# Attention with forgetting gates and a SwiGLU block on one core: fillers on their own tile, other heads' logs sent early, constants by ScalarE, a new order

## The chip, the cores and the metric

The kernel runs on one NeuronCore of one Trainium2 chip. A core has five engines with a program each: TensorE (PE, matmuls; its weight loads are shown apart as PEld), VectorE (DVE), ScalarE (ACT), GpSimd (POOL) and SyncE (SP). Each runs its program in order, and they wait for each other by semaphores. SP, ACT and POOL also issue DMA transfers. The metric is the device time of one execution in microseconds (us); lower is better. A time given for a kernel is the median of its runs.

## What is computed

The inputs are q, k and v of shape (8 batches, 8 heads, 576 positions, 64) and a gate f in (0.8, 1.0) of shape (8, 8, 576). The reference, cut to what matters:

```python
scores = (q @ k.transpose(0, 1, 3, 2)) / 8
cum = np.cumsum(np.log(np.clip(f, 1e-4, 1.0)), axis=-1)
scores = scores + cum[..., :, None] - cum[..., None, :]      # decay
scores = np.where(causal, -1e9, scores)                      # no later key
attn = softmax(scores)
x = (attn @ v).transpose(0, 2, 1, 3).reshape(4608, 512)
g = x @ w_gate                                               # 512 x 1536
out = (g * sigmoid(g) * (x @ w_val)) @ w_out                 # 1536 x 512
```

So attention gives 4608 tokens of 512 features, and a gated feed-forward block follows.

## The kernel before, in words

All matmuls are in bfloat16 with sums in float32. A planner written in Python (class `Plan`) holds every step as an operation with an engine, an estimated duration, its predecessors, the buffers that it takes and a key. It plays the program through once: whenever an engine is free, it takes the ready operation with the lowest key, and the instructions are recorded in that order. The table `ORDER` at the end gives most operations a key; `T_SW`, `TWARM`, `QUAD0` and other constants are the planner's estimates. Once recorded, the order on every engine and every DMA queue is fixed. The planner puts fillers on PE (`dummy`, L995) where it expects PE to wait: matmuls whose result nobody reads.

The feed-forward part works in nine tiles of 512 tokens. For each of twelve blocks of 128 hidden features, `gate` (L892) multiplies the tokens by w_gate and w_val, ACT takes a tanh (L896), DVE forms the product in two steps (L900, L903), and `project` (L907) sums over the blocks into the output (L911, L914). In the first tile the first four blocks are done in two halves of 256 tokens, so that they can begin before all of batch 0 is through attention. The weights come in chunks on POOL's queue; in the first chunk there are four blocks.

Attention works by heads. Keys lie on partitions, queries on columns; a head's causal scores fill four banks of at most 512 columns. PE forms the scores (`score2` for batch 0, L708 to L720; `score` for the others, L690), ACT takes the exp (`expo`, L724), POOL clears the part above the diagonal (`mask`, L733), PE multiplies by v with a column of ones (`weigh`, L747), DVE divides by that column's sum (L754, L759), PE transposes (`flip`, L764), and the result is put into xT, the transposed tokens (L325 or L323).

For batches 0 and 1, q and k are loaded four heads at a time in "quads" (`ld_quad`, L541) by POOL, transposed by PE (`turn_two`, L549, for batch 0; `turn`, L565, for batch 1) and copied to their place in QK by ACT or DVE (L323, L325: the straightenings). Later batches go through DRAM and a transposing DMA.

The gates: `gates` loads f of the first 16 heads into 64 partitions, four copies of 16 rows (`ld_f`, four transfers, two each from SP and ACT), clips it on DVE (L355), takes the log on ACT (L358) into 128 partitions, and DVE forms the running sum (L362) and splits it into three bfloat16 parts in KG (L367 to L378); the columns are done in two parts, 256 and 320. `up` (L382) and `choose` (L387, L389) make the query side of the decay. `dec_in` (L399) writes eight small pieces of KG as extra rows of QK for batch 1; four more small writes fill rows of ones from the tile `ones` (L477). The other 48 heads are loaded flat, 128 x 216; after clip and log, `regroup` writes them to DRAM (L352) and reads them back a head per row (L350); DVE sums (L362) and splits them (`later`), and they go to DRAM (`dec_out`) for batches 2 and on.

Several constants are written once: the small factors `ct` and `one`, the padding of PT (L462), the ones beside v in three buffers VB (L505, L507), and the tile `ones` (L466).

## Time and profile before

| | us |
|---|---|
| median of 3 runs | 383.37 |
| lowest and highest run | 382.79, 384.94 |
| the profiled execution | 382.61 |
| its span, first to last instruction | 380.9 |
| PE busy in the span | 372.1 |
| DVE, ACT, POOL busy | 218.8, 211.2, 141.2 |

A row of a timeline gives the start in us from the span's start, the length, the engine, the line, the operation, what is written and read, and the number of instructions merged; in brackets stands the idle time of the engine before it and what ended it. A matmul's length includes the time until its result is out, so that the lengths of neighbours overlap. A row of the table by stretch gives busy times in a window. The chain of work that ended last is followed back from the last instruction through what released each step.

### The profile page before, as it was taken

The page shows a single profiled execution, that of the slowest core. Times are in us where ns is not written, and L with a number is a line of the kernel's source. Part 1 is how long each engine was busy: PE and PEld are TensorE (multiplying, and loading weights), DVE is VectorE, ACT ScalarE, POOL GpSimd, SP SyncE. Part 2 cuts the span into 40 slices and gives each one's busy share as a digit, 9 for nine tenths or more (in the row PEclk, how much of TensorE's full clock was granted, in tenths as well). Part 3 has the DMA queues.
Part 4 walks back from the last instruction along what each step waited for, and adds up shares of the span by engine and source line. Part 5 has one row for each costly group of instructions (what it writes and reads, how often), then busy time and mean ns, then how long its engine had stood idle before and what let it go on. Part 6 is the DMA issues. An engine that isn't in the chain of part 4 may idle for free.

```text
span 380.9 us, 8367 instructions
## 1 busy us (share of the span) xinstructions
PE 372.1 (98%) x3127; PEld 206.4 (54%) x3127; DVE 218.8 (57%) x458; ACT 211.2 (55%) x433; POOL 141.2 (37%) x368
## 2 busy tenths in 40 slices
PE   5999999999999999999999999999999999999997
PEld 3668555555555555545554565555654444444444
DVE  7899794467616772387327651576327815743860
ACT  5999745266566574835674577547763323323322
POOL 8896446236443463526452356513430000000000
PEclk9999999999999999999999999999999999999999
DMA  9999997997588989999799979992321011002003
GB/s 129 187 194 201 211 209 150 167 235 143 117 194 162 207 130 161 206 188 183 129 203 203 178 123 187 234 220 55 94 74 45 0 57 55 0 29 83 3 0 111
DMA packets 125319, 51.96 MB, mean 136 GB/s; under 512 B 112110, under 2 KB 119726, under 8 KB 124510
## 3 DMA queue, kind: packets, MB, share of 16 engines
q1 hardware_dynamic: 108782, 36.18, 47.8%
q0 software_dynamic: 16288, 15.14, 26.6%
q8 instruction: 24, 0.39, 0.4%
q14 instruction: 17, 0.14, 0.1%
q10 hardware_dynamic: 208, 0.11, 0.1%
HBM read 38.56 MB, written 17.07 MB: 146 GB/s over the span
## 4 chain that ended last, share of the span: by engine, by line
PE 89%; DMA 5%; ACT 2%; DVE 2%; issue 1%; POOL 1%; DVEq 0%; POOLq 0%
PE ps L892 46%; PE ps L907 25%; PE ps L690 9%; PE ps L747 7%; DMA lnf_d<-ot 4%; DMA QK<-lnf_d 1%; ACT PT L724 1%; PE ps L995 1%; PE ps L708 1%; PE ps L764 0%; DVE th L900 0%; ACT QK L323 0%; POOL xT L541 0%; PE ps L549 0%; DVE QK L362 0%
## 5 line engine op out<-in xcount | busy, mean ns | idle before, releaser
L896 ACT ACTIVATE th<-ps 128x512 f32<-128x512 f32 (+1 forms) x112 | 65.1, 582 | 83.9 <-PE ps L892 82.8
L892 PE MATMUL ps<-xT,wg 128*128 128x512 bf16 (+1 forms) x448 | 111.4, 371 | 0.2 <-DVE th L900 0.2
L892 PE MATMUL ps<-xT,wv 128*128 128x512 bf16 (+1 forms) x448 | 111.4, 371 | 0.1
L900 DVE SCALAR_TENSOR_TENSOR th<-th,ps 128x512 f32<-128x512 f32 (+1 forms) x112 | 74.6, 666 | 60.2 <-ACT th L896 59.8
L907 PE MATMUL ps<-wo,hh 128*128 128x512 bf16 (+3 forms) x468 | 105.8, 362 | 0.0
L724 ACT ACTIVATE PT<-ps 128x512 bf16<-128x512 f32 (+2 forms) x192 | 91.7, 510 | 18.6 <-PE ps L690 12.1
L903 DVE TENSOR_TENSOR hh<-th,ps 128x512 bf16<-128x512 f32 (+1 forms) x112 | 74.7, 668 | 11.8 <-PE ps L892 0.9
L733 POOL TENSOR_SCALAR_AFFINE_SELECT PT<-PT 128x128 bf16<-128x128 bf16 (+1 forms) x192 | 53.2, 282 | 55.5 <-ACT PT L724 50.4
L892 PEld LDWEIGHTS <-wv 128*128 128x128 bf16 x448 | 42.7, 97 | 41.6 <-issue 0.5
L690 PE MATMUL ps<-QK 68*128 68x256 bf16 (+4 forms) x392 | 64.8, 260 | 0.1
L892 PEld LDWEIGHTS <-wg 128*128 128x128 bf16 x448 | 42.3, 97 | 40.5 <-issue 0.5
L907 PEld LDWEIGHTS <-hh 128*128 128x128 bf16 x468 | 41.2, 97 | 34.4
L733 POOL TENSOR_SCALAR_AFFINE_SELECT PTa<-PTa 128x256 bf16<-128x256 bf16 x64 | 26.5, 418 | 85.3 <-ACT PTa L724 84.1
L754 DVE RECIPROCAL rc<-ps 128x5 f32<-128x5 f32 (+2 forms) x68 | 12.9, 190 | 68.3 <-PE ps L747 68.1
L911 ACT ACTIVATE ot<-ps 128x512 f32<-128x512 f32 (+3 forms) x39 | 22.0, 565 | 45.2 <-PE ps L907 43.7
L747 PE MATMUL ps<-VB,PT 128*128 128x65 bf16 x768 | 45.1, 193 | 0.0
L747 PEld LDWEIGHTS <-PT 128*128 128x128 bf16 x768 | 36.8, 97 | 14.4 <-POOL PT L733 1.3
L690 PEld LDWEIGHTS <-QK 68*128 68x128 bf16 x392 | 31.4, 97 | 17.2 <-issue 0.4
L724 ACT ACTIVATE PTa<-ps 128x384 bf16<-128x384 f32 x64 | 30.8, 488 | 14.3 <-PE ps L690 13.2
L759 DVE TENSOR_TENSOR xn<-ps,rc 128x320 bf16<-128x320 f32 (+2 forms) x72 | 32.2, 453 | 2.1
L325 POOL CAST VB<-natv 128x512 bf16<-128x512 f32 (+1 forms) x32 | 19.7, 631 | 0.0
L747 PEld LDWEIGHTS <-PTa 128*128 128x128 bf16 x192 | 13.1, 97 | 11.3 <-issue 1.1
(71 smaller groups left out, 153.2 us busy)
## 6 DMA issues: line engine op xcount, KB each, us to landing
out_dram<-ot SPq DMA_DIRECT2D x35, 256.0 KB
natv<-in_v_dram SPq DMA_DIRECT2D x25, 256.0 KB
qk_d<-in_q_dram POOLq DMA_DIRECT2D x24, 144.0 KB, 3.8
qk_d<-in_k_dram POOLq DMA_DIRECT2D x24, 144.0 KB, 4.4
wg<-in_moe_w_gate_dram POOLq DMA_DIRECT2D x3, 512.0 KB, 12.1
wv<-in_moe_w_val_dram POOLq DMA_DIRECT2D x3, 512.0 KB, 13.5
wo<-in_moe_w_out_dram POOLq DMA_DIRECT2D x4, 384.0 KB, 16.7
xT<-in_q_dram POOLq DMA_DIRECT2D x4, 288.0 KB, 8.8
```

The costliest lines, as they stand in the source:

```text
L325: E[e].tensor_copy(dst, src)
L690: nc.tensor.matmul(s[:, c : c + w], QK[:KR, hqk[p].i, 1, j * S + kt * P : j * S + (kt + 1) * P], QK[:KR, hqk[p].i, 0, j * S + q0 : j * S + ...
L724: nc.scalar.activation(place(h, i)[:, OFFS[i] : OFFS[i] + c], ps(bs)[:, :c], AF.Exp, scale=0.125)
L733: nc.gpsimd.affine_select(out=d, in_=d, pattern=pat, compare_op=ALU.is_ge, fill=0.0, base=0, channel_multiplier=-1,)
L747: nc.tensor.matmul(o[:, lo : lo + D + 1], pt[:, c : c + P], VB[hvb[b].i][:, kt, hb, : D + 1], start=first and n == 0, stop=last and n == l ...
L759: nc.vector.tensor_mul(XN[bx.i][:, qb : qb + nq, j], o, r)
L892: nc.tensor.matmul(ps(bf)[:, :n], w[:, ko, fc * P : (fc + 1) * P], xT[:, ko, t0 : t0 + n], start=(ko == 0), stop=(ko == KD - 1))
L896: nc.scalar.activation(TH[bt.i][:, :n], ps(bf)[:, :n], AF.Tanh, scale=0.5)
L900: nc.vector.scalar_tensor_tensor(out=t, in0=t, scalar=1.0, in1=ps(bf)[:, :n], op0=ALU.add, op1=ALU.mult)
L903: nc.vector.tensor_mul(HH[bh.i][:, lo : lo + n], TH[bt.i][:, :n], ps(bf)[:, :n])
L907: nc.tensor.matmul(ps(bf)[:m, c], HH[hs[fc].i][:, lo : lo + m], wo[:, fc, c], start=(fc == 0), stop=(fc == KF - 1))
L911: nc.scalar.activation(OT[bo.i][:m, c], ps(bf)[:m, c], AF.Copy, scale=0.5)
```

## The change

Five things are changed together, and the table `ORDER` is replaced, so that the order on all engines and queues is another.

The fillers multiply a tile of their own, `idle`, which DVE sets to ones at the start, and not the identity that POOL makes. The planner may place them from 0.8 us on (`ID_AT`, before 2.72); there are 38 and not 22. f of the first 16 heads is read in two transfers, one from SP and one from ACT, each writing 32 partitions from the same 16 rows read twice. The write of the other heads' logs to DRAM has the key -50 and may be planned from 6 us on (before 1 and 21), the read back from 16 us on (before 27). The ones of `VB[1]`, its zeros, and the tile `ones` may be written by ScalarE, with an activation of scale 0 and the constant as bias (`fill32`), and are. The recorded order has POOL issue two quads of q, one of k, a block of v and the second quad of k first, then the rest of v, then a chunk of w_val and one of w_gate ahead of batch 1's quads. On SP the four writes of rows of ones and the logs' write now stand ahead of the eight writes of gate rows, and the logs' read after the fifth of these. PE does all transposes of batch 0 before the scores of the second pair of heads, and those of batch 1 after the first gate block. The number of useful matmuls is the same.

Estimates of the planner are changed too: PE's half speed counts for transposes and ends at 7.0 and not 7.5 us, transposes of batch 0 take 0.22 and not 0.41, f is delayed by 0.7 and not 0.2 after its issue, small SP writes take 0.64 and not 0.45. A second part of the cheaper gate rows for the scores (`ONEHOT1`, `QS[1]`) is written but empty.

```diff
-                        if o.tag[0] != "turn":
-                            dur *= self.clock(t)
+                        dur *= self.clock(t)
...
+    idle = sb("idle", [P, P], BF16)
...
-    QS = xT[:, 3, 3 * S + D : 3 * S + D + HALF]
+    QS = [xT[:, 3, 3 * S + D : 3 * S + D + HALF], xT[:, 0, 2 * S : 3 * S - HALF]]
...
-        E[e].dma_start(out=lf[2 * H * c : 2 * H * (c + 1)], in_=f.rearrange("b h s -> (b h) s")[: 2 * H])
+        src = bass.AP(f.tensor, f.offset, [[0, 2], [S, 2 * H], [1, S]])
+        E[e].dma_start(out=lf[4 * H * c : 4 * H * (c + 1)], in_=src)
...
-        lds = [op(("ACT" if n % 2 else "SP", 0.45), ld_f, n, key=-40, dma=0.1, packet=100, tag="f") for n in range(4)]
-        ld1 = op(("SP", 0.5), ld_f, None, key=-39, dma=LD1, packet=50, ready=LD1_AT, behind=lds[2:3], tag="f1")
+        lds = [op(("ACT" if n else "SP", 0.6), ld_f, n, key=-40, dma=0.2, packet=100, tag="f") for n in range(2)]
+        ld1 = op(("SP", 0.5), ld_f, None, key=-39, dma=LD1, packet=50, ready=LD1_AT, behind=lds[:1], tag="f1")
...
-        a = op(("SP", 0.5), regroup, False, after=[l1], key=1, dma=0.5, packet=40, ready=21, tag="regroup")
+        a = op(("SP", 0.5), regroup, False, after=[l1], key=-50, dma=0.5, packet=40, ready=6, tag="regroup")
         regrouped.append(a)
-        l1 = [l1, op(("SP", 0.5), regroup, True, after=[a], key=1, dma=0.4, packet=100, ready=27, tag="regroup")]
+        l1 = [l1, op(("SP", 0.5), regroup, True, after=[a], key=2, dma=0.4, packet=100, ready=16, tag="regroup")]
...
+    def fill32(e, t, x):
+        if e == "ACT":
+            z = ct[:, 0:1]
+            src = bass.AP(z.tensor, z.offset, [[z.ap[0][0], t.shape[0]]] + [[0, n] for n in t.shape[1:]])
+            nc.scalar.activation(t, src, AF.Copy, scale=0.0, bias=x)
+        else:
+            E[e].memset(t, x)
...
-            E[e].memset(ones.bitcast(F32), ONE2)
+            fill32(e, ones.bitcast(F32), ONE2)
...
-                nc.vector.memset(VB[what][:, :, :, D:].bitcast(F32), ONE2)
+                fill32(e, VB[what][:, :, :, D:].bitcast(F32), ONE2)
             if what:
-                nc.vector.memset(VB[0 if what == "rest" else what][LAST:, NB - 1], 0.0)
+                fill32(e, VB[0 if what == "rest" else what][LAST:, NB - 1].bitcast(F32), 0.0)
...
+    op(("DVE", 0.12), lambda e: nc.vector.memset(idle.bitcast(F32), ONE2), key=-1e5)
...
-    o_vb = [op(("DVE", 0.4 if i else 0.12), blank, i, key=(-29.5, VB1_KEY)[i] if i < FIRST else 40 + 2000 * i, ready=0 if i == 0 else 10 if i < FIRST else 15) for i in range(NVB)]
+    o_vb = [op({"DVE": 0.4, "ACT": 0.6} if i == 1 else ("DVE", 0.4 if i else 0.12), blank, i, after=[o_ct] if i == 1 else [], key=(-29.5, VB1_KEY)[i] if i < FIRST else 40 + 2000 * i, ready=0 if i == 0 else 4.5 if i < FIRST else 15) for i in range(NVB)]
...
-    o_ones = op(ONES, blank, "ones", key=ONES_KEY, ready=10)
+    o_ones = op(ONES, blank, "ones", after=[o_ct], key=ONES_KEY, ready=4.5)
...
-        nc.tensor.matmul(z[:, :HALF], ident, ident.unsqueeze(1).to_broadcast([P, 2, P]), start=True, stop=True)
+        nc.tensor.matmul(z[:, :HALF], idle, idle.unsqueeze(1).to_broadcast([P, 2, P]), start=True, stop=True)
...
-TWARM = 7.5
-ID_AT = 2.72
+TWARM = 7.0
+ID_AT = 0.8
...
-QUAD0 = (1.85, 1.25, 1.65, 1.4)
+QUAD0 = (1.55, 1.45, 1.5, 1.4)
...
+ONEHOT1 = ()
...
-ONES = ('DVE', 0.3)
+ONES = {'DVE': 0.3, 'ACT': 0.32}
...
 ORDER = {
-    0: -76.058, 1: -665.8079, 2: -126.6589, 3: -127.6642, 4: 17.8158, 5: -127.6652, 6: -370.9327, 7: -665.8069, 8: -315.3735,
+    0: -1162.0513, 1: 132.4814, 2: -34.2406, 3: -978.2224, 4: -24.6101, 5: -24.6111, 6: -185.9564, 7: 238.587, 8: 241.7308, 9: 245.9194,
...
```

More of the change, by code (lines that the diff above doesn't have):

```diff
@@ L188, in run @@
                         taken[k] += 1
-                        push(max(end + (0.2 if o.tag == "f" else 0.9), T_SW if e == "POOL" else 0.0), "queue", o)
+                        push(max(end + (0.7 if o.tag == "f" else 0.9), T_SW if e == "POOL" else 0.0), "queue", o)
                         push(busy[e], "wake", None)
@@ L216 @@
 PACE_A = 8.8
-PACE0 = 58.0
+PACE0 = 57.0
 LEAD = 14.0
@@ L381, in up @@
     def up(e, c):
-        nc.scalar.activation(QS, cum[:, c], AF.Copy, scale=8.0)
+        nc.scalar.activation(QS[c.start > 0], cum[:, c], AF.Copy, scale=8.0)
     def choose(e, jj, c):
@@ L434, in gates @@
             a = op(("DVE", 0.1 + w * 0.00155), low, c, after=[a], key=kk, tag="low")
-            u = op(("ACT", 0.15 + w / 1100), up, c, after=[s], key=kk, tag="up") if i == 0 and ONEHOT else None
-            done.append([[a, o_one, u] if jj in ONEHOT and not i else
+            u = op(("ACT", 0.15 + w / 1100), up, c, after=[s], key=kk, tag="up") if (ONEHOT, ONEHOT1)[i] else None
+            done.append([[a, o_one, u] if jj in (ONEHOT, ONEHOT1)[i] else
                          [a, op({"ACT": 0.26 + w / 1100, "DVE": 0.08 + w / 960}, choose, jj, c, after=[s, o_one], key=PICK_KEY[i][jj], tag=("pick", i, jj))]
@@ L642, in four @@
                 bt = Buf("t", ("f", TURN_F))
-                o2 = op(("PE", 0.41), turn_two, jj, x, bt, after=[o1[x], o_id], take=[bt], key=kk, tag=("turn", 0, jj, x))
+                o2 = op(("PE", 0.22), turn_two, jj, x, bt, after=[o1[x], o_id], take=[bt], key=kk, tag=("turn", 0, jj, x))
                 turns.append(o2)
@@ L714, in score2 @@
                 o, keys = ps(bs[u])[:, c : c + w], KG_ALL[r, kt * P : (kt + 1) * P]
-                if i or jj not in ONEHOT:
+                if jj not in (ONEHOT1 if i else ONEHOT):
                     nc.tensor.matmul(o, keys, QG[jj][r, q0 : q0 + w], start=False, stop=end)
@@ L719, in score2 @@
                     nc.tensor.matmul(o, keys, one[r, jj : jj + 1].to_broadcast([D, w]), start=False, stop=False)
-                    nc.tensor.matmul(o, ident[r, mine : mine + 1].to_broadcast([D, P]), QS[r, q0 : q0 + w], start=False, stop=end)
+                    nc.tensor.matmul(o, ident[r, mine : mine + 1].to_broadcast([D, P]), QS[i > 0][r, q0 - (HALF if i else 0) : q0 - (HALF if i else 0) + w], start=False, stop=end)
     def expo(e, h, i, bs):
@@ L828, in attention2 @@
                     segs = [x[2] for x in BANKS[i]]
-                    cost = mm(*segs) * (3 if not i and jj in ONEHOT else 2) + 0.105
+                    cost = mm(*segs) * (3 if jj in (ONEHOT1 if i else ONEHOT) else 2) + 0.105
                     gate_rows = [o_past] + dec0[0][jj] + (dec0[1][jj] if i else [])
```

4 lines of the change are left out of this document (2 added, 2 removed), and 103 rows, old and new, of the table ORDER.

## The prediction, made before the changed kernel was run

> **What bounds the kernel now.** I read the table of busy time by stretch first, then the timeline of each engine over the first 50 us, then the chain of work that ended last.
>
> ```profile
> 0.00:60.00 60.00, 53.88 (x742) 35.99 (x743) 51.09 (x156) 45.42 (x100) 42.42 (x95) 1.00 1.24 188
> 60.00:378.20 318.20, 318.18 (x2387) 170.37 (x2385) 167.68 (x303) 165.51 (x333) 98.75 (x274) 1.00 0.66 127
> 378.20:380.90 2.70, 0.00 (x0) 0.00 (x0) 0.00 (x0) 0.22 (x1) 0.00 (x0) 0.99 0.34 95
> ```
>
> Columns: stretch, length, then busy time of PE, PE's weight loads, DVE, ACT and POOL, the granted clock, DMA share and GB/s. From 60 us until PE's last instruction PE is busy for 318.18 of 318.20 us, and 2.7 us of last stores follow. The new order keeps the same useful matmuls, so nothing can be won after 60 us; it can only be lost there. What the change is worth is decided before 60 us, where PE is idle for 6.12 us, and part of what counts as busy is filler or waiting between short matmuls.
>
> ```profile
> 10.00:15.00 5.00, 4.47 (x125) 3.42 (x123) 4.76 (x13) 4.99 (x12) 3.95 (x6) 1.00 1.72 180
> 15.00:20.00 5.00, 4.79 (x80) 2.89 (x74) 3.15 (x28) 5.00 (x14) 4.96 (x12) 1.00 1.44 199
> 20.00:25.00 5.00, 4.77 (x92) 3.52 (x89) 4.84 (x16) 4.58 (x12) 4.98 (x16) 1.00 1.22 209
> 25.00:30.00 5.00, 5.00 (x106) 3.71 (x105) 4.60 (x11) 4.48 (x11) 4.64 (x14) 1.00 1.73 170
> 30.00:35.00 5.00, 4.89 (x76) 4.13 (x73) 4.84 (x13) 4.81 (x11) 3.52 (x8) 1.00 1.31 202
> ```
>
> From 10 to 20 us ACT is full (4.99 and 5.00 of 5), and POOL from 15 to 25 (4.96 and 4.98): exp, then mask, then PE. PE becomes the bound when the first gate matmul starts, at 24.07 us (the L892 row below).
>
> ```profile
> 4.50 2.53 PE L995 MATMUL ps<-ident 128*128 128x256 bf16 x11 [4.50 <-POOL ident masks.py:199]
> 6.95 0.99 PE L549 MATMUL ps<-ident,xT 64*64 64x64 bf16 x36
> ...
> 9.19 0.66 PE L549 MATMUL ps<-ident,xT 64*64 64x64 bf16 x36 [0.15 <-ACT ot L358]
> ...
> 11.79 0.34 PE L708 MATMUL ps<-QK 64*128 64x256 bf16 x4 [0.51 <-ACT QK L323]
> ...
> 24.07 1.04 PE L892 MATMUL ps<-xT,wg 128*128 128x256 bf16 x8
> ```
>
> ```profile
> 7.68 1.19 ACT L323 ACTIVATE QK<-ps 128x576 bf16<-128x576 bf16 x2 [1.55 <-PE ps L549]
> 8.76 0.38 ACT L358 ACTIVATE ot<-ot 128x216 f32<-128x216 f32 x1
> 9.16 1.28 ACT L517 ACT_TABLE_LOAD   x1
> 10.46 0.20 ACT L517 ACTIVATE warm<-warm 1x1 f32<-1x1 f32 x1
> 10.57 0.64 ACT L387 ACTIVATE xT<-xT,ct 128x320 bf16<-128x320 f32 x1
> ...
> 12.70 0.46 ACT L724 ACTIVATE PTa<-ps 128x384 bf16<-128x384 f32 x1
> ...
> 13.61 1.96 ACT L724 ACTIVATE PTa<-ps 128x384 bf16<-128x384 f32 x5
> ...
> 18.63 3.04 ACT L724 ACTIVATE PT<-ps 128x512 bf16<-128x512 f32 x7
> 21.50 0.75 ACT L323 ACTIVATE QK<-ps 64x640 bf16<-64x640 bf16 x1
> ```
>
> ACT waits 1.55 us for the first transposes (L549), because the fillers wait for the identity and run at 0.23 us each (2.53 over 11) until 6.95. From 7.68 to 22 us it has no gap.
>
> **The change, part by part.** *Fillers.* They now need only a memset of ones on DVE, among its first instructions, so they start near 1.5 us instead of 4.50. The 18 of the first block take 18 x 0.23 = 4.1 us if all are as slow as the eleven above, so they end by 5.6. The first transposes can then start when the first q block lands.
>
> ```profile
> DMA to landing us min/median/max: 4.8/4.8/4.8
> DMA to landing us min/median/max: 7.1/7.1/7.1
> ```
>
> These are the first quad load (issued 1.3 us, landed 6.1) and the fourth (issued 5.1, landed 12.2). First transposes: 6.15 us instead of 6.95, and 0.66 instead of 0.99 us if PE is by then as fast as at 9.19. [...]
>
> *Constants by ScalarE.* Three fills (the ones tile, 64x288, and VB1's 128x40 and 64x264) leave DVE and stand on ACT between the logs and the first straightening. The nearest ACT row is the log of 216 columns, 0.38 us; the bounds for the three together are 0.60 (three times the 1x1 row, 0.20) and 1.14 (three times 0.38). I take 1.0, near the upper end, since two of the three are longer than 216 columns. It fits in the 1.55 us of waiting above, of which 0.8 goes because the transposes come earlier; 0.25 us is left over and pushes the straightenings. [...]
>
> *Order of the start.* The POOL queue now issues q, q, k, then a block of v, then k, where v stood second. The same five transfers precede the last k, so it lands again near 12.2: 6.1 us for the four after the first. A tenth less, 11.6, is the early end. ACT then runs, end to end: the logs until 5.7, fills and L382's copy until 7.1, four straightenings of 0.55 (two of 1.19 overlap) until 9.3, the log of 216 columns 0.35, the L387 pick 0.6, the Exp load 1.4 with its dummy, and a straightening 0.55, so 12.2. The last straightening needs the last k: 12.2 + 0.66 for its transposes, then 0.55: 13.4, with 12.9 as the lower end; I take 13.2. From there only exps follow. Before, the run of exps began at 13.61 with one already done. So on ACT the first exp is late (13.2 against 12.70), but the first gate now comes after 22 exps with nothing between. Twenty of them took 21.50 - 13.61 = 7.9 us, 0.395 each; 22 take 8.7. First gate: 13.2 + 8.7 = 21.9, with 0.3 for its bank and waits 22.2 us, against 24.07: 1.9 us earlier.
>
> PE has done less by then. Before, 18 transposes of batch 1 (L565) and 8 more L747 matmuls stood ahead of the first gate; now they follow.
>
> ```profile
> L565 PE MATMUL ps<-ident,xT 128*64 128x128 bf16 x72 | 3.2, 223 | 0.1
> L747 PE MATMUL ps<-VB,PT 128*128 128x65 bf16 x768 | 45.1, 193 | 0.0
> ```
>
> 18 x 3.2 / 72 = 0.8, and 8 x 45.1 / 768 = 0.5: 1.3 us that PE must still do once it is the bound. Net gain of the start: 1.9 - 1.3 = 0.6 us.
>
> *Straightenings put off.* Three copies of batch 1 on DVE and one on ACT (the 0.75 us row at 21.50) move behind the gate: 3.0 us. From 25 to 35 us DVE has 0.40 + 0.16 free and ACT 0.52 + 0.19, 1.27 together; ACT also arrives 1.9 us earlier. 3.0 - 1.27 - 1.9 is below nothing, so I take 0.1 us. Without that cover the price is 3.0 - 1.27 = 1.7.
>
> *Other heads' logs early.* The log of the other 48 rows goes to DRAM and back so that the running sum can be taken row by row.
>
> ```profile
> 24.04 13.71 DMA lnf_d<-ot
> 37.75 0.02 issue
> 37.77 4.79 DMA QK<-lnf_d
> 42.55 0.02 issue
> 42.58 1.37 DVE QK L362
> ```
>
> ```profile
> 40.00:45.00 5.00, 4.83 (x28) 2.43 (x27) 3.35 (x6) 3.14 (x7) 1.74 (x3) 1.00 1.23 216
> 45.00:50.00 5.00, 4.80 (x29) 2.38 (x28) 4.96 (x9) 2.67 (x7) 4.42 (x8) 1.00 1.22 214
> ```
>
> DVE stands idle until 42.58 and is then full (4.96 of 5) with the sum and its splits between the gate's L900 and L903, so PE loses 0.17 + 0.20 us. With the write issued near 10 us and the read at about 17, the data is there at 38, from which the order allows the sum. It can save from 0 to 0.37; I take 0.3, as DVE was idle for more than the sum's 1.37 between 38 and 42.6 (5 - 3.35 in its stretch). Moved ahead, the two transfers pass SP's queue: the read stands before three of the eight small writes of gate rows, so SP waits there if the write is late (a rival below).
>
> *f in two transfers.* One issue less on SP and on ACT; the clip is then bound by DVE's constants, which come 0.1 to 0.3 us later for the extra memset. At nothing: hidden by the ACT chain, which needs the last k anyhow. If it weren't, 0.3 us.
>
> Edits with one answer: the planner's constants and `QS` with a second half change no instruction (`ONEHOT1` is empty). Sixteen more fillers stand where PE waits; four after the first scores could cost up to 0.23 us each, 0.9; I count 0.1.
>
> **Sum**: 0.6 + 0.3 - 0.1 - 0.1 = 0.7 us less. The profiled execution took 382.61 us (span 380.9 and 1.7 around it); 381.9 by it. The median of the runs is 383.37, 0.76 above it, so 382.6 us in the median. What a measurement of this kernel tells from no change is about 0.5%, 1.9 us: I forecast no change, on its faster side. Its own range, from the bounds above: all of 1.9 and 0.37 with nothing lost gives 381.1; 0.9 for fillers, 0.25 for the fills and nothing from the logs gives 383.9.
>
> **Rivals.** *A: the whole start counts.* The 1.3 us of work put off fall into PE waits that stay in the 25 to 50 us stretches (0.11 + 0.17 + 0.20 idle, and waits between short matmuls). Then 1.9 + 0.37: 381.1 us, faster. For it: PE after 24 us isn't yet free of short waits. Against it: PE shows 5.00 of 5 from 25 to 30.
>
> *B: the straightenings starve PE (the other side).* DVE is at 4.60 and 4.84, ACT at 4.48 and 4.81 of 5 from 25 to 35; the copies hold PSUM banks that gate and scores need, and PE is in order. It decides once the free 1.27 us are used up before batch 1's first scores. Price: 3.0 us behind, none covered, less the 0.3 of the logs and the 0.6 of the start: 383.37 + 2.1 = 385.5 us.
>
> *C: SP waits for the logs' write.* If that write takes the 13.71 us it took before, it lands at 24, and three gate-row writes of batch 1 go out behind it, about 2 us later than now. Price at most 2.0 - 0.9: 384.5. Against it: then it stood behind two large loads of v, now behind four small writes.
>
> *D: PE is slow again after the early fillers.* Between 5.6 and 12 us PE has gaps of up to about 1 us that were filled before. Four groups of transposes at 0.99 instead of 0.66 and the first scores as much again: 2 x 4 x 0.33 = 2.6, so 383.37 + 2.6 - 0.9 = 385.1. [...]
>
> **How the numbers follow.** Forecast 0.50, A 0.22, B 0.15, C 0.06, D 0.05, other 0.02. Faster by over 0.5% means under 381.45: A and a tenth of the forecast's share, 0.26. Slower means over 385.3: B, some of D and the rest, 0.19. Same: 0.55. The range takes in A with 0.5 to spare and B: 380.5 to 385.5.
>
> **What would show it.** First transposes near 6.2 and the first gate near 22.2 us in PE's timeline; exps without gaps from 13.2 on ACT; DVE without the wait for the logs near 42; PE idle before 60 us near 5.4 less the new fillers. PE gaps of 0.3 us or more between 25 and 40 ended by DVE or ACT copies mean B; a late last gate row on SP means C; filler or transposes at the slow duration after 6 us mean D. New idle time on PE after 60 us would make all of it wrong.

## The result, and the profile after

| | before | after |
|---|---|---|
| median of 6 runs, on the same chip (us) | 382.80 | 387.18 |
| lowest and highest | 381.77, 384.94 | 386.34, 387.38 |
| the profiled execution, its span | 382.61, 380.9 | 386.51, 384.8 |

The changed kernel takes 1.0103 times as long (95% interval 1.0075 to 1.0131): slower by 1%, 4.4 us. I had forecast 382.6 us, and the range ended at 385.5. Of 31 executions of the kernel before that were timed beside the run with the early logs, six show a lower mean granted clock (0.991 or 0.996) and took 386.2 to 387.3 us, so that the ratios below, which take such executions in, come out lower than the medians alone would give.

The first view is the timeline of VectorE and ScalarE in the changed kernel: start, length, engine and line, and in brackets the idle time and what ended it.

```profile
6.89 0.89 DVE L356 TENSOR_SCALAR xT<-xT 64x256 f32<-64x256 f32 x2 [3.22 <-DMA xT<-in_f_dram]
...
7.21 1.86 ACT L359 ACTIVATE xT<-xT 64x256 f32<-64x256 f32 x4 [3.62 <-DVE xT L356]
...
13.43 1.28 ACT L527 ACT_TABLE_LOAD   x1
...
17.08 0.65 ACT L323 ACTIVATE QK<-ps 128x576 bf16<-128x576 bf16 x1 [1.63 <-PE ps L559]
17.63 1.64 ACT L734 ACTIVATE PTa<-ps 128x384 bf16<-128x384 f32 x4
```

The first clip waits until 6.89 us for f. In the kernel before it stood here:

```profile
3.58 0.35 DVE L355 TENSOR_SCALAR xT<-xT 64x256 f32<-64x256 f32 x1 [0.41 <-DMA xT<-in_f_dram]
```

Everything that hangs on f is 3.3 us late. The first exponential comes at 17.63 us, not at 13.2 as I had it. TensorE's timeline in the changed kernel:

```profile
1.42 4.02 PE L1005 MATMUL ps<-idle 128*128 128x256 bf16 x18 [1.42 <-DVE idle L522]
8.68 0.95 PE L559 MATMUL ps<-ident,xT 64*64 64x64 bf16 x36 [3.23 <-DMA xT<-in_q_dram]
...
13.55 1.89 PE L1005 MATMUL ps<-idle 128*128 128x256 bf16 x8
15.37 0.43 PE L718 MATMUL ps<-QK 64*128 64x256 bf16 x4
...
16.38 0.66 PE L559 MATMUL ps<-ident,xT 64*64 64x64 bf16 x36
...
27.22 0.60 PE L902 MATMUL ps<-xT,wg 128*128 128x256 bf16 x4
```

The fillers do start at 1.42 us, but then TensorE idles for 3.23 us until the first q lands, which it does at 8.6 us and not at 6.1. The first gate starts at 27.22 us; before, at 24.07. The table by stretch of the changed kernel (columns as in the prediction):

```profile
5.00:10.00 5.00, 1.76 (x41) 0.95 (x38) 2.75 (x8) 2.67 (x8) 4.23 (x6) 0.88 1.34 192
10.00:15.00 5.00, 4.79 (x84) 3.44 (x84) 3.62 (x8) 4.96 (x10) 2.90 (x4) 0.50 1.92 175
...
25.00:30.00 5.00, 5.00 (x98) 3.57 (x97) 3.34 (x13) 4.65 (x13) 4.98 (x16) 1.00 1.77 207
30.00:35.00 5.00, 5.00 (x113) 3.97 (x110) 4.84 (x11) 4.93 (x10) 4.54 (x12) 1.00 1.41 189
```

Two things are seen. From 10 to 15 us the granted clock is 0.50 (1.00 before in that stretch). And from 25 to 35 us TensorE is full, so the straightenings that the new order puts there starve nothing. Of the 3.9 us that the span is longer, 3.15 are lost before the first gate (27.22 for 24.07) and are not made good; the other 0.8 lie behind it, with 357.6 us from the first gate to the end where there were 356.8.

### The profile page after: what moved, and what is told of

It is laid out like the page before. It is cut to its first block, busy times and chain, and to the rows that moved or that the text cites. A ratio compares the mean times of both kernels' runs of the same rounds, so it can differ in the third digit from the quotient of the medians.

```text
span 384.8 us, 8336 instructions
## 1 busy us (share of the span) xinstructions
PE 373.6 (97%) x3096; PEld 208.7 (54%) x3143; DVE 216.2 (56%) x455; ACT 214.0 (56%) x437; POOL 139.9 (36%) x368
## 4 chain that ended last, share of the span: by engine, by line
PE 92%; ACT 3%; DMA 2%; issue 1%; POOL 0%; DVE 0%; SPq 0%; DVEq 0%; ACTq 0%
PE ps L902 48%; PE ps L917 23%; PE ps L700 10%; PE ps L757 7%; DMA xT<-in_f_dram 2%; ACT QK L323 2%; PE ps L1005 1%; PE ps L774 1%; DMA out_dram<-ot 1%; PE ps L718 1%; PE ps L559 1%; ACT xT L359 0%; PE ps L726 0%; PE ps L575 0%; ACT PT L734 0%
## 5 line engine op out<-in xcount | busy, mean ns | idle before, releaser
L902 PE MATMUL ps<-xT,wg 128*128 128x512 bf16 (+1 forms) x435 | 109.9, 371 | 0.7
L902 PE MATMUL ps<-xT,wv 128*128 128x512 bf16 (+1 forms) x432 | 109.4, 371 | 0.8
L917 PE MATMUL ps<-wo,hh 128*128 128x512 bf16 (+3 forms) x450 | 102.3, 362 | 0.9
L734 ACT ACTIVATE PT<-ps 128x512 bf16<-128x512 f32 (+2 forms) x192 | 91.6, 513 | 17.4 <-PE ps L700 10.9
L743 POOL TENSOR_SCALAR_AFFINE_SELECT PT<-PT 128x128 bf16<-128x128 bf16 (+1 forms) x192 | 52.4, 280 | 55.8 <-ACT PT L734 50.9
L700 PE MATMUL ps<-QK 68*128 68x256 bf16 (+4 forms) x392 | 64.0, 261 | 0.5 <-DVE rc L764 0.3
L757 PE MATMUL ps<-VB,PT 128*128 128x65 bf16 x768 | 43.7, 193 | 0.1
L757 PEld LDWEIGHTS <-PT 128*128 128x128 bf16 x768 | 35.9, 97 | 12.4 <-issue 0.5
L757 PEld LDWEIGHTS <-PTa 128*128 128x128 bf16 x192 | 13.2, 97 | 12.3 <-POOL PTa L743 1.4
```

What stands on the lines that cost most here:

```text
L700: nc.tensor.matmul(s[:, c : c + w], QK[:KR, hqk[p].i, 1, j * S + kt * P : j * S + (kt + 1) * P], QK[:KR, hqk[p].i, 0, j * S + q0 : j * S + ...
L734: nc.scalar.activation(place(h, i)[:, OFFS[i] : OFFS[i] + c], ps(bs)[:, :c], AF.Exp, scale=0.125)
L743: nc.gpsimd.affine_select(out=d, in_=d, pattern=pat, compare_op=ALU.is_ge, fill=0.0, base=0, channel_multiplier=-1,)
L757: nc.tensor.matmul(o[:, lo : lo + D + 1], pt[:, c : c + P], VB[hvb[b].i][:, kt, hb, : D + 1], start=first and n == 0, stop=last and n == l ...
L902: nc.tensor.matmul(ps(bf)[:, :n], w[:, ko, fc * P : (fc + 1) * P], xT[:, ko, t0 : t0 + n], start=(ko == 0), stop=(ko == KD - 1))
L917: nc.tensor.matmul(ps(bf)[:m, c], HH[hs[fc].i][:, lo : lo + m], wo[:, fc, c], start=(fc == 0), stop=(fc == KF - 1))
```

## Experiments: f's transfers

The changed kernel with four transfers of 16 rows, the order of all else the same:

```diff
-        src = bass.AP(f.tensor, f.offset, [[0, 2], [S, 2 * H], [1, S]])
-        E[e].dma_start(out=lf[4 * H * c : 4 * H * (c + 1)], in_=src)
+        for r in (2 * c, 2 * c + 1):
+            E[e].dma_start(out=lf[2 * H * r : 2 * H * (r + 1)], in_=f.rearrange("b h s -> (b h) s")[: 2 * H])
```

> The changed kernel, but each of its two f steps issues two transfers of 16 rows as before; every other instruction and its order is as in the changed kernel. Theory F (the doubled 32-row read of f is slow and holds up the first quads): the clip starts near 3.6 us instead of 6.89, the first q lands near 6.2 instead of 8.63, the first gate starts near 23 us instead of 27.22, and the time is 381.5 to 383.5 us. Rival O (the new order starves PE, straightenings put off, whatever f does): the clip comes early too, but the time stays at 385 us or more, with PE gaps between 25 and 40 us.

Measured: 384.70 us (383.85 to 385.44), ratio to before 1.0032 (1.0003 to 1.0061). The opposite edit, the kernel before with the two doubled transfers and nothing else changed:

```diff
-        E[e].dma_start(out=lf[2 * H * c : 2 * H * (c + 1)], in_=f.rearrange("b h s -> (b h) s")[: 2 * H])
+        if c > 1:
+            return
+        src = bass.AP(f.tensor, f.offset, [[0, 2], [S, 2 * H], [1, S]])
+        E[e].dma_start(out=lf[4 * H * c : 4 * H * (c + 1)], in_=src)
```

> The kernel before, with the one change that f comes in two transfers of 32 rows from the same 16 rows read twice; the order of everything else is as before. Theory F: clip near 6.9 us, first q near 8.6, and 2.5 to 4.5 us more than before, 385.5 to 387.5. Rival O: within 1 us of before.

Measured: 387.71 us (387.33 to 388.21), ratio 1.0113 (1.0063 to 1.0164): this part alone makes the old kernel 5.1 us slower. Not all of that is f's own lateness. TensorE waited 1.49 us for the first q and then stayed slow until about 20 us: 36 transposes took 0.99 us each time (0.66 in the kernel before from 9.19 us on), and four scores 0.50 us, for 0.34 before.

```profile
8.47 0.99 PE L552 MATMUL ps<-ident,xT 64*64 64x64 bf16 x36 [1.49 <-DMA xT<-in_q_dram]
...
18.41 0.50 PE L711 MATMUL ps<-QK 64*128 64x256 bf16 x4
```

The granted clock is given as 1.00 there all the same: the trace's first record of the clock begins at 20.23 us, and what lies before the first record counts as 1.00. In the early stretches the durations tell the clock, then, and not the column. What the late f and the slow TensorE cost apart from each other was not measured.

And two transfers of 32 rows each that read 32 different rows:

```diff
-        src = bass.AP(f.tensor, f.offset, [[0, 2], [S, 2 * H], [1, S]])
-        E[e].dma_start(out=lf[4 * H * c : 4 * H * (c + 1)], in_=src)
+        E[e].dma_start(out=lf[4 * H * c : 4 * H * (c + 1)], in_=f.rearrange("b h s -> (b h) s")[: 4 * H])
```

> The changed kernel with two transfers of 32 rows, but from 32 different rows of f, a plain two-dimensional read (the gates of batches 0 and 1 are then partly those of other heads, so this leaves out the second copy of the right rows). If the size or the number of transfers makes f slow, the clip starts near 6.9 us as in the changed kernel and the time is near 387; if it is the shape of the doubled read (outer step of two), the clip starts near 3.6 us and the time is within 1 us of the kernel with four transfers.

Measured: 384.88 us in one run, like the four transfers. So here it was neither the number nor the size of the transfers, but the doubled read. The clip's row in these three, in this order:

```profile
3.87 0.61 DVE L356 TENSOR_SCALAR xT<-xT 64x256 f32<-64x256 f32 x2 [0.20 <-DMA xT<-in_f_dram]
```

```profile
6.96 0.53 DVE L358 TENSOR_SCALAR xT<-xT 64x256 f32<-64x256 f32 x1 [3.80 <-DMA xT<-in_f_dram]
```

```profile
3.58 0.65 DVE L355 TENSOR_SCALAR xT<-xT 64x256 f32<-64x256 f32 x2
```

The view of the DMA queues shows how. Up to 7 us, ScalarE's queue moved the same 0.07 MB of f in 34 packets in the changed kernel (first fence) and in 64 in the kernel before (second):

```profile
q10 hardware_dynamic: 34, 0.07, 4.4%
```

```profile
q10 hardware_dynamic: 64, 0.07, 3.1%
```

The packets are 32 rows of 2,304 bytes and 2 packets of 4 bytes now; before, two times 16 rows and 16 packets of 4 bytes. With 32 different rows in one transfer they are 32 and 16, 48 in all. In the changed kernel ScalarE's rows start two at a time, from 2.38 to 4.79 us, and SyncE's follow, two at a time, from 4.73 to 6.23 us; the 32 different rows all start between 2.21 and 2.55 us. The queue of q, k and v lands some 2 us later too (first q at 8.6 for 6.1 us, last k at 14.0 for 12.3), and its packets show where: of the sixteen packets of 4 bytes that close the first q, fourteen have gone by 6.28 us, and the last two go at 8.19 and 8.30 us. With f in four transfers all sixteen go between 5.19 and 5.73 us. The counts of 2 and 16, the rows two at a time and the two late packets of q would fit a doubled read that goes out over two paths where the plain one has sixteen, and q's last two packets behind it on these two. That is my estimate from the packets; the trace does not name the DMA engines, and it was not shown.

## Experiments: fillers and clock in the new order

With f repaired, 2 us are left. Fillers on the identity again, all else as in the kernel with f in four:

```diff
-        nc.tensor.matmul(z[:, :HALF], idle, idle.unsqueeze(1).to_broadcast([P, 2, P]), start=True, stop=True)
+        nc.tensor.matmul(z[:, :HALF], ident, ident.unsqueeze(1).to_broadcast([P, 2, P]), start=True, stop=True)
```

> The changed kernel with f in four transfers as in the first of these runs, and the fillers multiplying the identity again, at the same places of the order (so the first of them waits for POOL until about 4.3 us). It prices the fillers' own tile alone. As predicted, the own tile lets the first transposes start near 6.2 us at 0.66 us each, against near 8 with the identity (18 fillers of 0.23 from 4.3); ACT is then bound by the last k anyhow, so 0 to 1 us slower than the first of these runs. Rival: the identity is as good or better (0 to 1 us faster), as fillers that end later keep PE fast.

Measured: 384.76 us (383.74 to 385.04), no difference. But two effects cancel. With the tile of ones (f in four, TensorE's timeline):

```profile
6.08 0.66 PE L559 MATMUL ps<-ident,xT 64*64 64x64 bf16 x36 [0.63 <-DMA xT<-in_q_dram]
6.67 0.39 PE L1005 MATMUL ps<-idle 128*128 128x256 bf16 x2
7.54 0.96 PE L559 MATMUL ps<-ident,xT 64*64 64x64 bf16 x36 [0.48 <-DMA xT<-in_q_dram]
8.43 0.61 PE L1005 MATMUL ps<-idle 128*128 128x256 bf16 x4
9.76 0.99 PE L559 MATMUL ps<-ident,xT 64*64 64x64 bf16 x36 [0.72 <-DMA xT<-in_k_dram]
10.68 1.89 PE L1005 MATMUL ps<-idle 128*128 128x256 bf16 x8
12.50 0.50 PE L718 MATMUL ps<-QK 64*128 64x256 bf16 x4
...
14.11 0.99 PE L559 MATMUL ps<-ident,xT 64*64 64x64 bf16 x36
```

The first transposes are at 6.08 us and take 0.66 us, as predicted. Then, at 9.09 us, the granted clock falls to 0.50, after gaps of 0.63 and 0.48 us and at the start of one of 0.72 us, and eight slow fillers (1.89 us) delay the first score. With the identity the first block ends at 8.41 us, after the landing, and the first transposes take 0.99 us; but all later ones take 0.66, and the clock does not fall.

In the next kernels the planner's sequence is recorded first and changed before it is emitted. `BRIDGE` gives the number of fillers in each block that the planner had. First only the 18 of the first block are kept:

```diff
-                    o.fn(e)
+                    self.log.append((o, e))
...
+    log, blocks = [], []
+    for o, e in plan.log:
+        if e is None:
+            if not log or log[-1][1] is not None:
+                blocks.append(o)
+                log += [(o, None)] * (BRIDGE[len(blocks) - 1] if len(blocks) <= len(BRIDGE) else 0)
+            continue
+        log.append((o, e))
+    for o, e in log:
+        o.fn(e) if e else dummy(o)
...
+BRIDGE = (18,)
```

> The changed kernel with f read again in four transfers of 16 rows, and of its fillers only the 18 of the first block: the 20 later ones (2, 4, 8, 2, 2, 1 and 1) are left out, the order of all else is the same. Theory one (the 2 us that the change loses beside f's transfers are lost between 10 and 16 us: the fillers stand ahead of the first score and of the last k's transposes on TensorE, which takes its work in order, and all exponentials stand behind that k's straightening on ScalarE): the first score starts at about 11.6 us instead of 12.50, the last k's transposes at about 12.6 instead of 14.11, still at 0.99 us since the clock stays at one half, the first exponential at about 14.3 instead of 15.69, and the time is 383.4 us, some 1.3 less than with the fillers. Theory two (the straightenings that the new order leaves for the time between 25 and 40 us starve TensorE there): the early gain is given back, and the time stays at 384.7 us. If the clock needs the later fillers, it comes back later than 15.92 us, and part of the 1.3 us is not seen.

Measured: 383.96 us (383.49 to 384.88), ratio 1.0024 (1.0002 to 1.0046): 0.7 us less by the medians, which were taken on two chips and whose runs overlap. The first score came at 11.55, the last k's transposes at 12.62 and the first exponential at 14.19 us. Next, fillers only in the first four waits for landings, as many as fill them (the blocks had 18, 2, 4 and 8):

```diff
-BRIDGE = (18,)
+BRIDGE = (23, 6, 13, 6)
```

> The same, with the fillers put where TensorE waits for landings alone: 23, 6, 13 and 6 in the first four blocks (before the first, second and third transposes, and before the first score), none after them. Theory one: TensorE has no gap over 0.2 us before 11 us, the granted clock is 1.0 from about 5.4 us on and doesn't fall, the transposes take 0.66 us, the first score starts at about 11.3 us, the last k's transposes right at its landing near 12.0, the first exponential at about 13.3, and the time is 382.4 us, level with the kernel before. Theory two: 384.5 us.

Measured: 383.92 us (383.20 to 385.74). The clock does not fall, all transposes take 0.66 us, and it gains nothing over half clock. The kernel before with early fillers on the tile of ones:

```diff
-        nc.tensor.matmul(z[:, :HALF], ident, ident.unsqueeze(1).to_broadcast([P, 2, P]), start=True, stop=True)
+        nc.tensor.matmul(z[:, :HALF], idle, idle.unsqueeze(1).to_broadcast([P, 2, P]), start=True, stop=True)
...
-ID_AT = 2.72
+ID_AT = 0.8
```

> The kernel before with one part of the change: its fillers multiply the tile of ones and may start at 0.8 us, so that 20 instead of 11 stand ahead of the first transposes; order and transfers are the old ones. My theory: the first block runs from 1.4 to 5.9 us, the first transposes start at the landing of q, 6.12 us, at 0.66 instead of 0.99 us, and since ScalarE's and VectorE's chains come later than that, the time is 382.4 us, the same within 0.3. The rival: the clock window that follows holds gaps of TensorE and the clock falls to one half as in the changed kernel, and the time is 384 us or more.

Measured: 384.42 us (382.44 to 384.82), ratio 1.0002 (0.9961 to 1.0043), so not told apart as a whole. But the runs fall apart by their mean granted clock: the six with 0.987 took 384.42 to 384.82 us and one with 0.991 383.75, the three with 1.000 took 382.44, 382.50 and 383.72. The profiled one is of the first kind:

```profile
5.00:10.00 5.00, 2.63 (x81) 1.84 (x79) 4.79 (x11) 3.85 (x7) 5.00 (x8) 0.85 1.37 169
10.00:15.00 5.00, 5.00 (x87) 3.50 (x84) 3.84 (x11) 3.71 (x8) 3.82 (x6) 0.50 1.72 181
15.00:20.00 5.00, 5.00 (x78) 3.49 (x75) 2.14 (x20) 4.02 (x10) 2.88 (x7) 0.62 1.44 198
```

In the old order the half clock costs about 2 us, then, and it comes in most runs and not in all.

## Experiments: what else holds the new order up

Two steps of the new order undone, each from the kernel with few fillers. The first two exponentials go ahead of the last k's straightening (`move` puts an operation right behind another):

```diff
+    move(("exp", 0, 0), ("str", 0, 1, 1))
+    move(("exp", 4, 0), ("exp", 0, 0))
```

> The kernel with few fillers (f in four transfers, 18 fillers), with one step of the new order undone on ScalarE: the first two exponentials (heads 0 and 4) go ahead of the last k's straightening instead of behind it. Theory one (ScalarE stands idle for 1.3 us in front of that straightening, since it takes its work in order and the last k is the last to land; whatever is lost before the first gate comes out at the end one to one): the first exponential starts at about 12.8 us instead of 14.19, ScalarE's idle time between 10 and 15 us falls from 1.27 to about 0.2 us, the first gate comes about 0.9 us earlier than 23.78, and the time is about 383.0 us, 0.9 less than the 383.96 of the kernel with few fillers. Theory two (the start is slack, and the order after 25 us sets the end): 383.9 us.

Measured: 384.13 us (383.57 to 384.86). The first exponential did come at 12.91 us, and the time did not move. In the profiled execution TensorE was slow for longer (four scores still took 0.53 us at 15.43, for 0.33 at 15.31 with few fillers), ScalarE waited for it twice behind the first two exponentials (0.42 and 0.47 us), and the first gate came at 24.42 us, later than 23.78. The logs late again:

```diff
+    log.insert(1 + max(n for n, x in enumerate(log) if x[1] and x[0].tag == "decin"), there)
+    log.insert(min(n for n, x in enumerate(log) if x[1] and x[0].start > 31.7), back)
```

> The kernel with few fillers, with the other heads' logs sent to DRAM late again, behind the small SBUF transfers, and read back where the kernel before reads them. If the early logs pay in the new order as they do in the old one (0.7 us there), this takes 384.6 us; if the new order has no use for them, 383.9 us.

Measured: 384.10 us (383.65 to 384.72): in this order no gain from the early logs is seen. Then the full clock and the early exponentials together (the bridging blocks with 26, 6, 12 and 6 fillers, and the two moves above):

> The new order with f in four transfers, the fillers only where TensorE waits for landings (26, 6, 12 and 6 in the first four blocks) so that the clock stays at 1.0, and the first two exponentials ahead of the last k's straightening. If TensorE at half clock is what made the early exponentials worthless, they now pay: first exponential at about 12.8 us, third at about 13.9, ScalarE's idle time under 0.5 us between 10 and 20 us, first gate at about 23.0 us, time 383.0 us, 0.9 less than with either step alone (383.92 and 384.13). If GpSimd's transfers and masks set the first gate, it stays near 23.8 us and the time near 383.9 us.

Measured: 383.98 us (383.33 to 384.88). The profiled execution, the longest of the ten, has a stop in TensorE's timeline:

```profile
14.05 0.27 PE L729 MATMUL ps<-one,xT 64*128 64x256 bf16 x1
14.09 0.21 PE L718 MATMUL ps<-QK 64*128 64x128 bf16 x1
15.01 0.27 PE L730 MATMUL ps<-xT,ident 64*128 64x256 bf16 x1 [0.69 <-issue]
```

"issue" means that the engine waited for nothing that the profile shows. ScalarE loses 1.16 us by it. The kernel with fillers on the identity has the same stop, later and longer:

```profile
17.09 0.27 PE L730 MATMUL ps<-xT,ident 64*128 64x256 bf16 x1 [1.13 <-issue]
```

So has the one with bridging fillers (0.35 us, at 14.72). In all of them it is the 224th matmul that the trace records, whatever stands there. The view of the DMA queues of the kernel above, from 12 to 14 us, has this row:

```profile
q8 instruction: 1, 0.02, 3.2%
```

That is one transfer of 16,384 bytes of program, which began at 12.71 us and took 1.04. The kernels at half clock fetch such a block too, and so does the kernel before (at 13.58 us), and they do not stop. But in every run kept here the 224th matmul starts 2.3 us or more after that transfer begins: 2.30, 2.35, 2.42 and 2.55 us in the four that stop, 2.31 (early logs alone), 2.45 (the kernel before) and up to 5.9 us in the others. That would fit a supply of instructions for which TensorE has to wait if it comes to that place too early: my guess from these times, which no run shows directly. To test it, half as many fillers of twice the length:

```diff
-        nc.tensor.matmul(z[:, :HALF], idle, idle.unsqueeze(1).to_broadcast([P, 2, P]), start=True, stop=True)
+        nc.tensor.matmul(z[:, :MT], idle, idle.unsqueeze(1).to_broadcast([P, 4, P]), start=True, stop=True)
...
-BRIDGE = (26, 6, 12, 6)
+BRIDGE = (13, 3, 6, 3)
```

> The kernel with bridging fillers and the exponentials ahead, with fillers of 512 columns, half as many (13, 3, 6 and 3 for 26, 6, 12 and 6), so that TensorE's stream is 46 instructions shorter before the first score. If the supply of instructions makes TensorE stop, the stop of 0.69 us at 14.32 us goes, or comes later and is shorter, ScalarE's idle time between 10 and 20 us falls from 1.17 us to about 0.5, the first gate comes about 0.5 us earlier than 23.73, and the time is about 383.4 us (383.98 with the short fillers). If the stop has another reason, it stays at the same operation, the third scores, and the time stays at 384.0 us.

Measured: 383.20 us (382.86 to 383.66), ratio 0.9978 (0.9940 to 1.0017), the lowest time of the new order, and not told apart from the kernel before (382.91 beside it). The stop is gone, and the 224th matmul starts 2.83 us after the transfer begins. Later, at 16.28 us, TensorE waits 0.52 us for a mask, and the first gate starts at 23.35 us, 0.38 earlier than with the stop. ScalarE goes through until 14.19 us and then waits 0.28 us for TensorE, for 1.16:

```profile
12.46 0.83 ACT L734 ACTIVATE PTa<-ps 128x384 bf16<-128x384 f32 x2
13.20 0.62 ACT L323 ACTIVATE QK<-ps 128x576 bf16<-128x576 bf16 x1
13.73 0.46 ACT L734 ACTIVATE PTa<-ps 128x384 bf16<-128x384 f32 x1
```

Three transfers of batch 1's v off GpSimd's way, behind the masks, beside bridging fillers and early exponentials:

```diff
+    for n, behind in ((1, ("mask", 5, 3)), (2, ("v", 1, 1)), (0, ("v", 1, 2))):
+        move(("v", 1, n), behind)
```

> As the first of these, and the three transfers of the next batch's v behind the masks too. If GpSimd sets the first gate in the new order, 1 us less than without this step, 382 us or a little more; if not, the same as without it, or more if v comes late.

Measured: 384.78 us (384.27 to 387.54), 0.8 more than without: TensorE stops for 0.96 us for "issue" and for 0.8 us more at a mask that now stands behind the three transfers.

One number holds these kernels together. In seven of the nine kernels of the new order with f in four transfers (f alone, identity, few fillers, bridging fillers, early exponentials, late logs, long fillers), the first gate starts anywhere from 23.35 to 25.59 us, and from there to the end of the span are 358.1 to 358.2 us each time; in the other two there are 359.1 and 359.4. In the kernel before there are 356.8. So the new order has 1.3 us more behind its first gate and needs a gate that much earlier to draw level; the best one was 0.7 earlier.

## Experiments in the old order

The early logs alone, the kernel before otherwise (the write right behind the log, the read behind the last of the eight writes of gate rows):

```diff
+    log.insert(1 + max(n for n, x in enumerate(log) if x[1] and x[0].tag == "ln1"), there)
+    log.insert(1 + max(n for n, x in enumerate(log) if x[1] and x[0].tag == "decin"), back)
```

> The kernel before with one part of the change: the other heads' logs go to DRAM right after they are computed, ahead of the small SBUF transfers on SP's queue, and come back after the last of the first eight of them; all else is as it was. My theory: nothing waits for these transfers, 382.6 us, the same within 0.3. The rival (SP's queue waits for the write and holds the rows of the second half up): 384 us or more.

Measured: 382.08 us (381.82 to 382.84) against 382.81, ratio 0.9966 (0.9934 to 0.9997). It is faster than both expectations, and the only kernel here whose interval lies below the kernel before. TensorE is full where it was not (4.83 and 4.80 of 5 before):

```profile
40.00:45.00 5.00, 5.00 (x30) 2.62 (x29) 4.79 (x9) 4.36 (x10) 1.53 (x5) 1.00 1.24 206
45.00:50.00 5.00, 5.00 (x38) 2.64 (x36) 4.77 (x8) 1.94 (x5) 3.68 (x7) 1.00 1.25 225
```

Four tries to go further from there. The exponentials' table loaded in ScalarE's early wait:

```diff
+    move("clip1", "scan", 0)
+    move("ln1", "up")
+    log.insert(at("ln1") + 1, table)
```

> The kernel before with the early logs, and with the clipping and the log of the other heads put right behind the first scan, so that ScalarE loads the table for the exponentials in its idle 1.55 us after 6.13 us instead of at 9.16 us. Transfers, fillers and TensorE's order are the old ones. Theory: ScalarE's gapless stretch after 9 us loses 1.7 us of work, but the last two straightenings of q are then bound by the landing of the second q at 10.6 us, so that the first exponential comes at about 12.2 instead of 12.68 us; the gain is handed through to the end: 381.5 us. If TensorE's or VectorE's work sets the first gate instead, 382.1 us as with the early logs alone.

Measured: 382.44 us (381.88 to 385.21), ratio 0.9998 (0.9973 to 1.0022). ScalarE's wait moved from before the table to after it (1.46 us idle between 10 and 15 us), and the first exponential came at 12.64. With scores and exponentials moved ahead of what waits for the second q and k:

```diff
+    move(("s2", 0, 0, 0), ("str", 0, 0, 1))
+    move(("exp", 0, 0), ("s2", 0, 0, 0))
+    move(("exp", 4, 0), ("exp", 0, 0))
+    move(("s2", 0, 1, 0), ("str", 0, 2, 0))
+    move(("exp", 5, 0), ("s2", 0, 1, 0))
```

> The same, and the scores of the first two pairs of heads and three exponentials moved ahead of what waits for the second q and k: the first score right behind the first k's straightening, at about 10.5 us instead of 11.79, the first two exponentials at about 11.1 us, ahead of the second q's straightenings. Theory: ScalarE then has no gap from 9.9 us on, the first gate comes about 1.5 us earlier than 24.07, and the time is about 380.8 us, less than both kernels. If exponentials this early only wait later (for the second k, which lands at 12.26 us, or for values of v), 382 us.

Measured: 383.80 us (382.40 to 385.82). The first exponential came at 11.76 us, the first gate at 24.55, later than 24.07. The profiled execution took 382.42 us, close to the lowest, so it does not show what the slower ones lost. GpSimd did not follow; its timeline there:

```profile
12.66 1.39 POOL L541 DMA_DIRECT2D xT<-in_q_dram  x2 [1.00 <-DMA xT<-in_k_dram]
14.05 0.43 POOL L733 TENSOR_SCALAR_AFFINE_SELECT PTa<-PTa 128x256 bf16<-128x256 bf16 x1
```

The first mask stands behind two transfers that GpSimd issues, and these behind a landing. So two masks ahead of them:

```diff
+    move(("mask", 0, 0), ("exp", 4, 0))
+    move(("mask", 4, 0), ("mask", 0, 0))
```

> The old order with early logs, early table load and early exponentials (383.80 us so), with the masks of heads 0 and 4 put ahead of three transfers of the next q and k on GpSimd. If GpSimd sets the first gate: its first mask starts at about 12.3 instead of 14.05 us, its wait of 1.0 us ahead of those transfers is filled with the two masks, the first gate comes about 0.9 us earlier than 24.55, and the time is about 382 us. If ScalarE sets it, nothing changes: 383.5 us.

Measured: 384.27 us (382.56 to 385.83). The masks came at 12.47 us; q and k of batch 1 went out up to 0.9 us later for it, and in the profiled execution the clock fell to 0.66 between 15 and 20 us, so that this run does not tell the masks' worth. And the three transfers of v behind the masks, early logs alone otherwise:

```diff
+    for n, behind in ((1, ("mask", 2, 2)), (2, ("v", 1, 1)), (0, ("v", 1, 2))):
+        move(("v", 1, n), behind)
```

> The old order with early logs (382.08 us so), with three transfers of the next batch's v, which GpSimd issues between 16.9 and 20.5 us in 0.89 us each, put behind the masks of the first heads, at about 20.5 us. If GpSimd sets the first gate, it comes at about 23.0 instead of 24.07 us (ScalarE's exponentials bind from there), and the time is about 381.3 us, unless v then comes late for the second batch, near 35 us, which would show as TensorE waiting for VB. If ScalarE sets the first gate, 382.1 us.

Measured: 384.09 us (383.82 to 385.35), 2.0 more. The three take 2.66 us together from 23.81 us, and the masks behind them hold TensorE up:

```profile
27.73 0.39 PE L747 MATMUL ps<-VB,PT 128*128 128x65 bf16 x7 [1.86 <-POOL PT L733]
```

The transfers cost GpSimd's time wherever they stand; between the first masks, where they were, they cost less than behind them.

## Why the prediction was wrong

- *f in two transfers* is the step that failed: "At nothing: hidden by the ACT chain, which needs the last k anyhow. If it weren't, 0.3 us." It cost 2.5 us in the new order (387.18 to 384.70) and 5.1 in the old one, there with TensorE slow until about 20 us. I counted issues, and not how the rows go out: two at a time, from 2.38 to 6.23 us, where 32 different rows all start between 2.21 and 2.55. The cover failed as well: the chain's last k came later itself (14.0 for 12.3 us), as the first q did.
- *Fillers after the first scores*: "could cost up to 0.23 us each, 0.9; I count 0.1". All 20 later fillers together measured 0.7 by the medians; mis-sized.
- *Rival D* was real, and its chance of 0.05 too small. The granted clock fell to 0.50 after gaps of 0.63 and 0.48 us with f repaired, and after one of 3.23 us in the changed kernel itself. How long a gap it takes is not shown, and runs of one kernel differ: in the kernel before with early fillers the mean granted clock was 0.987 in six runs and 1.000 in three. The rival's price, 2.6 us, is near the 2 us of the old order; in the new one a full clock by itself gained nothing.
- *First gate at 22.2*: "from there only exps follow". With f, fillers and clock repaired the exponentials began at 12.46 us, before the 13.2 of the prediction, and the gate came at 23.35: 10.9 us from the first exponential to the gate, one straightening of 0.62 among them, for the 8.7 and 0.3 of the sum. The start gained 0.7 us at best, for the 1.9 forecast. The chain is not ScalarE's alone: in other variants TensorE was slow or stopped for "issue", and GpSimd's masks wait behind its transfers. The 1.3 us put off behind the gate were right (358.1 less 356.8). With all this repaired the change comes out at +0.3 us by the medians, with an interval that holds zero, for the -0.7 of the sum.
- *First transposes at 6.15 and 0.66 us*: right once f is repaired (6.08, 0.66).
- *Logs early*: 0.3 predicted from waits of 0.37; 0.7 by the medians in the old order, nothing seen in the new one. Rival C is refuted by the first of these, where it was tried.
- *Straightenings put off*, 0.1, and rival B: TensorE was full from 25 to 35 us in the changed kernel, and its only wait listed between 24 and 60 us is 0.3 us, for VectorE's reciprocal and not for a copy, so the small price was right and the rival wrong.
- *Constants by ScalarE* were not tried by themselves: the three took 1.13 us there (0.42 and 0.71) for the 1.0 of the prediction.
- A small slip in the chances changes nothing: 0.22 for A and a tenth of 0.50 are 0.27, not 0.26.

By the medians 4.3 of the 4.4 us are 2.5 for f's read, 0.7 for late fillers, 0.8 between the kernel with few fillers and the one with long ones, and 0.3 that is within the interval; 0.1 is the difference between two medians of the kernel before. The 0.8 came only with the full clock and the early exponentials and without the stop: with the clock alone or the exponentials alone, or these two, TensorE's half clock or its stop took the place of the other. Open stays what sets the time from the start of the fetch to the end of the stop: the transfer itself had ended 1.3 to 1.6 us before TensorE went on, and two kernels that came to that place after 2.31 and 2.45 us did not stop.

## What to carry to other kernels

Look at the shape of the read before merging two transfers into one: a read repeated by an outer step of 2 reached its user 3.3 us later than two plain ones. Where TensorE starts slow, read its clock from durations until the profile has a record of it (from 20.23 us on in the kernel before with the doubled read, where 36 transposes took 0.99 us at 8.47 us, for 0.66 in the kernel before at 9.19). Compare the time from a fixed mark, here the first gate, to the end: it tells work put off from work saved. A filler is not free where an engine takes its work in order: it belongs in front of a wait for a landing, long rather than many (20 later ones cost 0.7 us by the medians; with 25 long ones for 50 short the time was 383.20 us for 383.98). And a change of parts is to be measured part by part: the early logs, worth 0.7 us alone in the old order, did not show in a change that lost 4.4.

## What was not expected of the hardware

- A transfer of 72 KB in 32 rows, its source repeated by an outer dimension of 2, went out in 34 packets, two rows at a time, where 32 different rows took 48; the work that needed it began 3.3 us later.
- The granted clock fell to 0.50 after gaps of TensorE of 0.63 and 0.48 us (f in four transfers). In the kernel before with early fillers its mean was 0.987 in six runs of ten and 1.000 in three.
- With the doubled read in the old order TensorE ran at its slow durations until about 20 us, in stretches for which the profile gives a granted clock of 1.00.
- At full clock TensorE stopped for 0.35 to 1.13 us at the 224th matmul of its program, near a transfer of 16,384 bytes of instructions; with 25 fewer fillers in front, twice as long, it did not.
